# Attention and two feed-forward layers on one core: weight conversions later, and a small add moved from VectorE to GpSimd

## The chip, the cores and the metric

The kernel runs on one core of a Trainium2 chip. The metric is device time in microseconds (us), as the median over runs. TensorE is called PE, VectorE DVE, ScalarE ACT, GpSimd POOL and SyncE SP in the profile, and PEld is TensorE's weight load. A line such as L500 is a line of the kernel before, whose numbers the profile uses.

## The reference

Causal attention with a decay is computed for 4 batches of 8 heads, 576 positions of width 64. Its output, 2304 tokens of width 512, goes through two feed-forward layers.

```
cum    = cumsum(log(clip(f, 1e-4, 1)))            # per head
scores = q @ k.T / 8 + cum[i] - cum[j], masked above the diagonal
e      = exp(scores - rowmax);  attn = e / (sum(e) + 1e-9)
x      = attn @ v                                 # 2304 x 512
y      = (sigmoid(x @ w_gate) * (x @ w_val)) @ w_out      # d_ff 1536
h      = y @ w_in
out    = (h * clip(h + 3, 0, 6) / 6) @ w_out2             # d_ff 2048
```

Here q, k and w_gate are drawn with larger spreads (factors of about 6, 6 and 3.7).

## The kernel before

**Attention.** Two heads of a batch make a pair; there are 16 pairs. Each pair has four units, one for each group of query rows (unit 1 holds two blocks of 128 rows, units 2 and 3 one each, unit 4 the last 64 rows of both heads), so there are 64 units. The main loop has a step t for each unit, and three more. Step t does, in this order: `fixed(t)`, which puts on TensorE, in an order written by hand, the opening of the score banks with a mask, the transposes (`tt`, L220) of the exponentials of unit t-3, the scores (`st`, L216) of unit t, preparation of the next pair's q and k, at most one group of the first feed-forward layer, and, once in a pair, the product with v (`pv`); then `expo(t)`, where VectorE adds the decay to the scores and takes the row minimum (L500) and ScalarE takes the exponential with its sum (L508); then `norm(t)`, below, for unit t-1. Three PSUM banks hold scores, and a unit needs two, so TensorE can open a unit's banks only when VectorE has read (L500) the first bank of the unit before.

**Normalising.** For unit t-1, VectorE adds 1e-9 to the sums (L543, one to four columns of 128 partitions), takes the reciprocal (L544), and GpSimd multiplies the exponentials by it (L546). L543 and L544 are ordered behind VectorE's last read of the scores of unit t, at high priority. `pace["dve"]`, the reciprocal, is what a weight conversion is ordered behind.

**Weight conversions.** Weights of the first layer are read as 64-bit numbers of an odd layout and turned into a high and a low float32r part. The work comes in halves (`Half`) of 128x512 elements: a DMA of 512 KB (L101), four steps to float32 (L107, L108 and L114 on VectorE, L111 on ScalarE between the last two), then the high part (L64 on GpSimd, or L62 on ScalarE) and the low part (L65 on GpSimd). `Converter.run(n, engs)` adds n to a credit and issues one half whenever the credit reaches 1. It is called at the end of each step from t = 4, with `EA` (high part on GpSimd) below t = 16 and `EF` (high part on ScalarE) from there. The first 12 halves are those of the first two groups of 256 features (gate, value, gate, value, out, out: two halves each); when they are done the rate falls to `CS`.

**Filling.** From t = 23 on, `fill.one()` puts one group of the first layer's matmuls (12 of 128x128 by 512) into a step, except mostly the one with `pv`. Three chunks of tokens take 12 groups each: 8 of gate and value (`pg`, `pv`) and then 4 of the product with w_out (`po`). A group whose weights are not converted yet is not issued, and the step stays without one. What is left of the 36 groups after the last unit is issued then, back to back, ahead of the rest of the first layer and the second.

The order on SP's queue is that of the issues; a load that waits for a store holds back the loads behind it. For engines other than TensorE a planner orders instructions by priority and its own estimate of times, and `keep_in_program_order` binds TensorE's.

Of the kernel before, what the change touches and what calls it, by code (L numbers as in the profile page):

```python
# [12 lines left out]
ALU = mybir.AluOpType  # L13
# [7 lines left out]
def attn_moe_kernel(  # L21
# [13 lines left out]
    nc = tc.nc  # L35
# [7 lines left out]
    NQ = 4  # L43
# [150 lines left out]
    conv = Converter()  # L194
# [110 lines left out]
    def behind(i):  # L305
        return tc.issue_after(i.ins) if i is not None else ExitStack()
# [14 lines left out]
    class Pair:  # L321
# [217 lines left out]

        def norm(self, s):  # L540
            m, n = self.m[s], len(self.es[s])
            with behind(reads[-1]), tc.high_priority():
                nc.vector.tensor_scalar(m[:, 8 : 8 + n], m[:, 4 : 4 + n], 1.0e-9, None, ALU.add)  # L543
                pace["dve"] = nc.vector.reciprocal(m[:, 12 : 12 + n], m[:, 8 : 8 + n])  # L544
            for j, e in enumerate(self.es[s]):
                pace["pool"] = nc.gpsimd.tensor_scalar(e, e, m[:, 12 + j : 13 + j], 1.0, ALU.mult, ALU.mult)  # L546
# [504 lines left out]
    class Second:  # L1051
# [93 lines left out]
        def unit(self, k, x, ys, temps, between={}):  # L1145
            u1, u2, p5 = temps
            g, tt = self.ga[k % 2], nc.vector.tensor_tensor
            r11, r22, r12 = self.act(u1, g, 0, 0), self.act(p5, g, 1, 1), self.act(u2, g, 1, 0)
            r21 = self.act(x(), g, 0, 1)
            then = {1: (r11,), 2: (r11,), 3: (r11,), 4: (r22,), 5: (r12, r22, r22), 6: (r21, r12, r12, r21, r21)}  # L1150
            for s in range(7):
                if s in (1, 3):
                    y = ys.pop(0)()
                o = y if s % 2 else x()
                self.product(o, k, s, s in (0, 1, 3))
                if s in (0, 2, 3):
                    nc.scalar.copy({0: u1, 2: u2, 3: p5}[s], o)  # L1157
                elif s < 6:
                    c = {1: u1, 4: p5, 5: u2}[s]
                    tt(c, c, o, ALU.add)  # L1160
                for r in then.get(s, ()):
                    next(r)
                if k % NQ2 == NQ2 - 1:
                    self.load_block(k // NQ2 * 7 + 7 + s)
                if s in between:
                    between[s]()
# [72 lines left out]
    EA = (nc.scalar, nc.gpsimd, nc.gpsimd)  # L1239
    EF = (nc.scalar, nc.scalar, nc.gpsimd)  # L1240
    WU = (8, 4, 4, 4)

    KD, KT, RT = 4, 7, 0

    CA, C0, CB, CC = 0.65, 4, (1.8, 1.0, 1.5, 1.7, 2.0), 1.0

    CE, CS = 0.38, 0.12


    NGA, NCA, GA = 2, 3, 1  # L1250

    NSA = 8
# [111 lines left out]
    for t in range(len(units) + 3):  # L1364
        for job in (fixed, expo, norm, prep):
            job(t)
        if t == 2:
            eight = ep.tile([P, S], F32, tag="e", name="eight")[: B * H]
            nc.vector.tensor_scalar(eight, cum, -8.0, 1.0, ALU.mult, ALU.mult)
            nc.sync.dma_start(cum_d[1], eight)  # L1370
        p, s = unit(t - 4)
        if p and s == p.order[-1] and p.hp == NP - 1 and p.b < NCA:
            done = p.b + 1
        p, s = unit(t - 5)
        if p and s == p.order[-1] and t < len(units) + 3:
            fill.load(p.b, p.hp + 1)
        if t >= C0:
            conv.run(CS if len(conv.jobs) <= 2 * NSA - 6 * NGA else CE if t < NQ * (KT - 1) else CA, EA if t < NQ * KD else EF)
        fill.n = done
    att.close()  # L1380
    pace["dve"] = None
# [63 lines left out]
```

## Time and profile before

| what | value |
|---|---|
| median of 3 runs | 1002.28 us (1002.18 to 1002.36) |
| the profiled execution's own time | 1003.57 us |
| its span in the trace | 1001.8 us |
| mean granted TensorE clock | 0.998 |
| busy share of the span | PE 98%, DVE 53%, ACT 48%, POOL 29% |

The span is from the first to the last instruction of the program on the core. A busy share is an average over stages; the attention stage covers about the first 278 us.

### The profile page before, as it was taken

The numbers are of one execution on the slowest core, as the hardware profiler recorded it, in microseconds if no ns is written. First come the engines' busy times: TensorE is split into PE (matmuls) and PEld (weight loads), VectorE is DVE, ScalarE is ACT, GpSimd is POOL, SyncE is SP. The second block draws the span as 40 slices with busy tenths as digits, with TensorE's granted clock in tenths as the row PEclk, the third lists the DMA queues.
The fourth block names the chain that finished last, engine by engine and source line by source line (L and its number), as shares of the span: only waits on it lengthen the run. The fifth ranks groups of instructions, "written<-read, shape, count | busy, mean of one in ns | idle before, by whom it ended". The sixth has DMA issues, their size and how long they took to land.

```text
span 1001.8 us, 16150 instructions
## 1 busy us (share of the span) xinstructions
PE 986.5 (98%) x5733; PEld 810.4 (81%) x5733; DVE 530.9 (53%) x1220; ACT 476.9 (48%) x1094; POOL 290.5 (29%) x360
## 2 busy tenths in 40 slices
PE   8889999999999999999999999999999999999998
PEld 4556766667688889988888888899899898998987
DVE  6777856645347543737777574553534443333322
ACT  6787677667634432424434343453444443433322
POOL 3675655545323220302334131111111111111110
PEclk9999999999999999999999999999999999999999
DMA  7999796744324352566977578654686845753211
GB/s 184 294 250 226 198 244 156 185 143 145 119 79 154 117 166 82 175 210 264 331 258 252 179 270 318 245 198 166 237 330 206 293 147 193 294 209 148 81 66 64
DMA packets 141072, 197.30 MB, mean 197 GB/s; under 512 B 84192, under 2 KB 93408, under 8 KB 136896
## 3 DMA queue, kind: packets, MB, share of 16 engines
q1 hardware_dynamic: 140944, 196.20, 59.9%
q8 instruction: 45, 0.74, 0.3%
q14 instruction: 35, 0.29, 0.1%
q10 hardware_dynamic: 48, 0.07, 0.0%
HBM read 142.88 MB, written 53.36 MB: 196 GB/s over the span
## 4 chain that ended last, share of the span: by engine, by line
PE 91%; DVE 3%; ACT 2%; DMA 2%; issue 1%; POOL 0%; SPq 0%; DVEq 0%; ACTq 0%; POOLq 0%
PE po L216 34%; PE pv L216 18%; PE u L216 17%; PE pg L216 15%; PE st L216 4%; PE tt L220 3%; DVE e L500 1%; DMA kn<-in_k_dram 1%; ACT e L508 1%; DMA cum_d<-eight 1%; DMA x_d<-x 0%; DVE raw L108 0%; ACT raw L111 0%; ACT etB L580 0%; PE o L216 0%
## 5 line engine op out<-in xcount | busy, mean ns | idle before, releaser
L216 PE MATMUL po<-w,big 128*128 128x512 f32 x864 | 200.5, 390 | 0.0
L216 PEld LDWEIGHTS po<-w,big 128*128 128x128 f32 x864 | 161.8, 188 | 32.8
L216 PE MATMUL pg<-big,wg 128*128 128x512 f32 (+1 forms) x720 | 161.9, 371 | 0.0
L216 PE MATMUL pv<-big,wv 128*128 128x512 f32 (+1 forms) x720 | 161.4, 371 | 0.0
L216 PE MATMUL po<-big,wo 128*128 128x512 f32 (+1 forms) x720 | 160.9, 371 | 0.2 <-DVE big L65 0.2
L216 PEld LDWEIGHTS pg<-big,wg 128*128 128x128 f32 x720 | 125.8, 189 | 27.2 <-issue 4.0
L216 PEld LDWEIGHTS pv<-big,wv 128*128 128x128 f32 x720 | 125.6, 189 | 26.8 <-issue 4.5
L216 PEld LDWEIGHTS po<-big,wo 128*128 128x128 f32 x720 | 125.6, 189 | 25.7 <-issue 2.2
L1160 DVE TENSOR_TENSOR h<-h,u 128x384 f32<-128x384 f32 x69 | 38.2, 554 | 154.0 <-PE u L216 154.0
L546 POOL TENSOR_SCALAR e<-e,m 128x256 f32<-128x256 f32 (+4 forms) x144 | 86.8, 617 | 48.8 <-DVE m L544 32.1
L508 ACT ACTIVATE e<-e,m 128x256 f32<-128x256 f32 (+4 forms) x144 | 83.6, 584 | 31.6 <-DVE m L500 20.3
L216 PE MATMUL u<-h,big 128*128 128x384 f32 x504 | 90.2, 336 | 0.4 <-DVE h L1160 0.4
L216 PE MATMUL u<-h,h 128*128 128x384 f32 x504 | 90.1, 336 | 0.0
L216 PEld LDWEIGHTS u<-h,big 128*128 128x128 f32 x504 | 88.3, 188 | 1.8 <-DVE h L1160 0.8
L216 PEld LDWEIGHTS u<-h,h 128*128 128x128 f32 x504 | 88.4, 188 | 1.0
L1109 POOL TENSOR_TENSOR big<-tail,big 128x384 fp32r<-128x384 f32 x30 | 30.5, 1018 | 196.5 <-PE u L216 115.5
L1157 ACT COPY h<-u 128x384 f32<-128x384 f32 x69 | 32.8, 475 | 111.5 <-PE u L216 111.5
L500 DVE CUSTOM_DVE_ANT_0 e<-st,dc 128x384 f32<-128x384 f32 (+3 forms) x110 | 53.5, 520 | 47.9 <-PE st L216 30.3
L872 DVE SCALAR_TENSOR_TENSOR sg<-sg,pv 128x512 f32<-128x512 f32 (+1 forms) x48 | 29.7, 618 | 92.3 <-PE pv L216 59.7
L111 ACT ACTIVATE raw<-raw 128x512 f32<-128x512 f32 x68 | 45.6, 682 | 67.1 <-DVE raw L108 64.5
L62 ACT CAST big<-sg 128x512 fp32r<-128x512 f32 (+1 forms) x60 | 34.8, 580 | 60.6 <-DVE sg L872 54.6
L114 DVE SCALAR_TENSOR_TENSOR raw<-raw 128x512 int32<-128x512 int32 x68 | 52.5, 782 | 19.4 <-ACT raw L111 18.9
(141 smaller groups left out, 1202.8 us busy)
## 6 DMA issues: line engine op xcount, KB each, us to landing
h<-xc_d SPq DMA_DIRECT2D x21, 768.0 KB, 7.2
big<-x_d SPq DMA_DIRECT2D x28, 512.0 KB, 5.8
raw<-in_moe_w_out_dram SPq DMA_DIRECT2D x28, 512.0 KB, 3.7
h<-wt_d SPq DMA_DIRECT2D x12, 1024.0 KB, 7.4
big<-wt_d SPq DMA_DIRECT2D x12, 1024.0 KB, 7.6
x_d<-x SPq DMA_DIRECT2D x16, 576.0 KB, 3.9
h<-wb_d SPq DMA_DIRECT2D x12, 768.0 KB, 4.6
big<-wb_d SPq DMA_DIRECT2D x12, 768.0 KB, 5.2
```

What stands on the lines that cost most here:

```text
L62: nc.scalar.copy(hi, src)
L111: nc.scalar.activation(e, e, AF.Copy, scale=2.0**-112)
L114: nc.vector.scalar_tensor_tensor(low, high, 3, low, ALU.logical_shift_left, ALU.bitwise_or)
L216: i = nc.tensor.matmul(*a, **k)
L220: i = nc.tensor.transpose(*a)
L500: i = nc.vector.tensor_tensor_reduce(out=e, in0=st, in1=d, op0=ALU.add, op1=ALU.min, scale=self.by, scalar=init, accum_out=m[:, a : a + 1],)
L508: nc.scalar.activation(e, e, AF.Exp, bias=m[:, a : a + 1], scale=-1.0, accum_out=m[:, 4 + b : 5 + b])
L546: pace["pool"] = nc.gpsimd.tensor_scalar(e, e, m[:, 12 + j : 13 + j], 1.0, ALU.mult, ALU.mult)
L872: pace["dve"] = nc.vector.scalar_tensor_tensor(sg, sg, 1.0, pv, ALU.add, ALU.mult)
L1109: (nc.vector if f else nc.gpsimd).tensor_tensor(lo, sg, hi.bitcast(F32), ALU.subtract)
L1157: nc.scalar.copy({0: u1, 2: u2, 3: p5}[s], o)
L1160: tt(c, c, o, ALU.add)
```

## The change

Two edits. The add of 1e-9 is issued on GpSimd, as a tensor_scalar with a multiplication by 1.0 behind the add, at high priority and without an order against VectorE's reads; the reciprocal stays on VectorE. The credit that `Converter.run` gets in a step is 0.24 in place of 0.38, and it changes to 0.65 from t = 21 in place of t = 24. The other rates stay.

```diff
         def norm(self, s):
             m, n = self.m[s], len(self.es[s])
+            with tc.high_priority():
+                nc.gpsimd.tensor_scalar(m[:, 8 : 8 + n], m[:, 4 : 4 + n], 1.0e-9, 1.0, ALU.add, ALU.mult)
             with behind(reads[-1]), tc.high_priority():
-                nc.vector.tensor_scalar(m[:, 8 : 8 + n], m[:, 4 : 4 + n], 1.0e-9, None, ALU.add)
                 pace["dve"] = nc.vector.reciprocal(m[:, 12 : 12 + n], m[:, 8 : 8 + n])
...
-    CE, CS = 0.38, 0.12
+    CE, CS, CT = 0.24, 0.12, 21
...
         if t >= C0:
-            conv.run(CS if len(conv.jobs) <= 2 * NSA - 6 * NGA else CE if t < NQ * (KT - 1) else CA, EA if t < NQ * KD else EF)
+            conv.run(CS if len(conv.jobs) <= 2 * NSA - 6 * NGA else CE if t < CT else CA, EA if t < NQ * KD else EF)
```

## Rows read from the trace of the kernel before

**Rows 1.** The page: busy time, share and instructions of TensorE.

```profile
PE 986.5 (98%) x5733; PEld 810.4 (81%) x5733; DVE 530.9 (53%) x1220; ACT 476.9 (48%) x1094; POOL 290.5 (29%) x360
```

**Rows 2.** Windows: length; busy PE, PEld, DVE, ACT, POOL; clock. Two early pairs; steps 32-34.

```profile
39.09:51.42 12.33, 10.11 (x105) 6.00 (x101) 11.22 (x41) 10.36 (x34) 10.19 (x15) 1.00 1.08 320
...
64.15:76.58 12.43, 10.80 (x114) 6.42 (x111) 10.74 (x40) 11.36 (x36) 8.87 (x12) 1.00 0.92 247
124.53:138.23 13.70, 13.47 (x107) 8.70 (x106) 8.16 (x35) 10.32 (x29) 8.15 (x15) 1.00 0.96 244
```

**Rows 3.** Waits of PE, then of PEld, 24 to 100 us (total, times, longest).

```profile
PE st L216 <- DVE m L500: 3.5, 6, 2.1
PE st L216 <- ACT raw L111: 2.5, 2, 1.4
...
PEld tt L220 <- POOL e L546: 2.3, 5, 0.8
```

**Rows 4.** Timeline (start, us, instruction [idle before]): TensorE opens score banks.

```profile
32.02 0.51 PE L216 MATMUL st<-masks,identb 128*128 128x384 bf16 x2 [2.06 <-DVE m L500]
...
48.18 0.29 PE L216 MATMUL st<-masks,identb 128*128 128x128 bf16 x2 [1.41 <-ACT raw L111]
...
58.19 0.50 PE L216 MATMUL st<-masks,identb 128*128 128x384 bf16 x2 [0.70 <-DVE m L500]
...
63.61 0.29 PE L216 MATMUL st<-masks,identb 128*128 128x128 bf16 x2 [0.18 <-DVE m L500]
...
73.64 0.29 PE L216 MATMUL st<-masks,identb 128*128 128x128 bf16 x2 [1.09 <-ACT raw L111]
```

**Rows 5.** Groups of VectorE, 24.57 to 85.75 us (busy us, mean ns; idle before).

```profile
L108 DVE SCALAR_TENSOR_TENSOR raw<-raw 128x512 int32<-128x512 int32 x7 | 5.9, 839 | 0.1
L114 DVE SCALAR_TENSOR_TENSOR raw<-raw 128x512 int32<-128x512 int32 x7 | 4.8, 692 | 2.2 <-ACT raw L111 2.2
L543 DVE TENSOR_SCALAR m<-m 128x2 f32<-128x2 f32 (+2 forms) x18 | 4.7, 263 | 0.0
...
L107 DVE TENSOR_SCALAR raw<-raw 128x512 int32<-128x512 int32 x7 | 2.9, 408 | 0.0
```

**Rows 6.** Timeline: VectorE idle before L500, units 9, 14, 17 and 22.

```profile
37.46 0.56 DVE L500 CUSTOM_DVE_ANT_0 e<-st,dc 128x384 f32<-128x384 f32 x1 [0.65 <-PE st L216]
...
52.99 0.69 DVE L500 CUSTOM_DVE_ANT_0 e<-st,dc 128x512 f32<-128x512 f32 x1 [1.40 <-POOL e L546]
...
62.99 0.56 DVE L500 CUSTOM_DVE_ANT_0 e<-st,dc 128x384 f32<-128x384 f32 x1 [0.96 <-POOL dt L386]
...
78.06 0.69 DVE L500 CUSTOM_DVE_ANT_0 e<-st,dc 128x512 f32<-128x512 f32 x1 [1.31 <-PE st L216]
```

**Rows 7.** Groups of GpSimd, whole span, shapes kept apart.

```profile
L546 POOL TENSOR_SCALAR e<-e,m 128x512 f32<-128x512 f32 x32 | 25.9, 823 | 6.9 <-DVE m L544 4.5 <-ACT etB L580 1.6 <-PE st L216 0.8
...
L546 POOL TENSOR_SCALAR e<-e,m 128x256 f32<-128x256 f32 x32 | 16.8, 524 | 0.0
```

**Rows 8.** Timeline: GpSimd's low part and VectorE's add at the same time.

```profile
58.18 1.30 POOL L65 TENSOR_TENSOR wv<-raw,wv 128x512 fp32r<-128x512 f32 x1
...
58.73 0.78 DVE L543 TENSOR_SCALAR m<-m 128x2 f32<-128x2 f32 x1
```

**Rows 9.** The chain that ended last: a group after the attention stage (start, us).

```profile
306.10 2.72 PE pg L216 x12
```

**Rows 10.** Timeline of PE: the first two `po` groups, steps 32 and 33.

```profile
126.03 2.80 PE L216 MATMUL po<-big,wo 128*128 128x512 f32 x10
...
129.74 0.59 PE L220 MATMUL tt<-ident,e 64*128 64x64 f32 x12
...
131.17 3.06 PE L216 MATMUL po<-big,wo 128*128 128x512 f32 x12
```

**Rows 11.** Groups of ScalarE, 24.57 to 85.75 us.

```profile
L111 ACT ACTIVATE raw<-raw 128x512 f32<-128x512 f32 x7 | 4.8, 690 | 3.0 <-DVE raw L108 3.0
...
L62 ACT CAST wg<-raw 128x512 fp32r<-128x512 f32 x2 | 1.4, 677 | 0.0
```

## The prediction, made before the change was run

> **What bounds the kernel now.** I began with the page's busy times: TensorE is busy 98% of the span, 986.5 of 1001.8 us [rows 1], so what can be won by removing waits is small. The windows show where the missing time lies. Two early pairs, steps 9 to 12 and 17 to 20, take 12.33 and 12.43 us, and TensorE's busy time in them is 10.11 and 10.80; at the same time VectorE has 11.22 and 10.74, ScalarE 10.36 and 11.36, GpSimd 10.19 and 8.87 [rows 2]. Here no engine is full and all are close: the pace is set by who waits for whom. The waits of TensorE in 24 to 100 us say for whom: 3.5 us for VectorE's L500, 2.5 us put down to ScalarE's L111, and its weight loads 2.3 us for GpSimd's multiplications [rows 3]. The 2.5 us are the same wait in disguise: both gaps stand before an opening of score banks (1.41 and 1.09 us), which needs L500, and L111 is what happened to end just then [rows 4]. From step 23 on, the groups of the first layer fill TensorE's stream, and there TensorE is the bound.
>
> So a saving before step 23 counts in full, as long as the next engine does not take it; one behind step 23 counts only where TensorE has nothing to fill in.
>
> **The change, part by part.** First the count, since the rates alone don't tell it. Adding the credit step by step, the halves are issued today at the end of steps 6, 9, 11, 14, 17, 19, 22, 24, 26, 27, 29 and 30; afterwards at 8, 12, 16, 20, 22, 23, 25, 27, 28, 30, 31 and 33. Before the first group at step 23 that is seven halves now and five then, and the twelfth comes three steps later. Each moved half takes its 512 KB load on SP's queue, three VectorE steps, L111 and the two parts with it.
>
> *(a) Early conversions.* One half costs VectorE 0.41 + 0.84 + 0.69 = 1.94 us [rows 5]. In today's kernel the four large gaps of TensorE before an opening, 2.06, 1.41, 0.70 and 1.09, each follow a conversion (those of steps 6, 11, 14 and 19), while an opening with none before it waits 0.18 [rows 4]. The excess is 5.26 - 4 x 0.18 = 4.5 us. The halves of steps 9 and 17 leave no such gap. Afterwards the first four halves all come at the first unit of a pair, where today none is. VectorE sits idle shortly behind these places for 0.65, 1.40, 0.96 and 1.31 us [rows 6], 4.3 us in all, against 4 x 1.94 = 7.8 us to place; 3.4 us are left, part of which falls in the pv groups' shadow, as for steps 9 and 17. I charge a third of it, 1.1 us: -4.5 + 1.1 = **-3.4 us**. Bounds: -4.5 (all hidden), and +3.0 (each of the four new places as dear as the dearest old one, 4 x (2.06 - 0.18) - 4.5).
>
> *(b) The add.* L543 takes 4.7 us in 18 instructions of the early stretch [rows 5]. TensorE waited for VectorE 6.0 us of 76 [rows 3], about a tenth, so I take a tenth: **-0.4 us**, with -4.7 as the lower bound, if all of it were on the path. GpSimd's price for an add on 1 to 4 columns is not in the trace; its multiplications of 512 and 256 columns take 823 and 524 ns [rows 7], a straight line that would leave 0.23 us at no columns. It is above nothing and below 0.52; I take 0.23. It adds a wait: the reciprocal now waits for GpSimd, and behind it on VectorE stand the next conversion and the next L500, for which TensorE waits. What hides it: the exponentials' sums are ready one unit before the reciprocal may run, since that is ordered behind L500 of the following unit. If the cover is gone, the cost goes to the five waits of the weight loads for GpSimd and their likes [rows 3]: 5 x 0.23 = 1.2 us as upper bound of the add's own time; a queue in front of it is a rival below. Past step 23 the add lies beside TensorE's groups, and its removal from VectorE too, so both are nothing there.
>
> One row bears on where the add lies: L543 took 0.78 us and ended with GpSimd's L65, which ran 58.18 to 59.48 beside it [rows 8]; the mean of 263 ns in this stretch [rows 5] holds such cases. The Trainium skill (SBUF — State Buffer, section "SBUF: two separate sides") says that the two engines share a port pair under an exclusive lock, held for a whole instruction. By that rule the add on GpSimd could itself hold up VectorE, at worst 18 x 0.23 = 4.1 us; a tenth of that would make this term 0.0 in place of -0.4. The rest of the sum stands without it.
>
> *(c) The hole in the filling.* Gate and value groups need halves 2, 4, 6 and 8, and by the count each finds them ready. The first po group needs the twelfth: today it is there for step 32, afterwards only for step 35 (34 holds pv). Steps 32 and 33 stay without a group, and two groups more are left for the end, 3 in place of 1, each at 2.72 us [rows 9]: +5.44. What the two steps give back is less than the groups' 3.71 (126.03 to 129.74) and 3.06 us [rows 10], as the other engines are now uncovered. The stretch of steps 32 to 34 takes 13.70 us; without the groups TensorE alone needs 6.9. ScalarE has 10.32 us of work there [rows 2], and the halves of steps 31 and 33 come in with 0.69 + 0.68 us each (L111 and L62 [rows 11]); less two copies out for the groups, of L62's size, that is 11.7. VectorE gets 8.16 + 2 x 1.94, less four adds of 0.26, 11.0. The nearest case is the early pace without groups, (12.33 + 12.43) / 8 = 3.1 a step [rows 2], 9.3 for three. It saves 4.4: 5.44 - 4.4 = **+1.0 us**. Bounds: -1.4 (6.9) and +3.4 (11.7).
>
> Loads: two fetches fewer sit on SP's queue before step 23 and two more at steps 31 and 33, ahead of loads that a pair needs a unit or more later. At the end, two chunks' loads of the next tokens wait for the last gate group, which comes two steps later; three left-over groups (8.2 us) cover them. I cost this at nothing; uncovered, it would be one load's landing, below the bounds above.
>
> Sum: -3.4 - 0.4 + 1.0 = -2.8 us, from the profiled execution's 1003.57 to 1000.8; that execution lies 1.3 above the median, so the median goes from 1002.28 to **999.5 us**.
>
> **The rivals.**
> *Other engines take the early gain.* ScalarE has 11.36 of 12.43 us in the pair of steps 17 to 20 [rows 2], and TensorE's weight loads already wait for GpSimd; against it, its own waits are mostly for VectorE. If only a third of (a) stays, -1.1 - 0.4 + 1.0 = -0.5: 1001.8 us.
> *The hole takes it all.* ScalarE's 11.7 us set steps 32 to 34: -3.8 + 3.4 = -0.4: 1001.9 us. For it speaks that two conversions fall right there; against it, that exponentials run two units ahead of their transposes.
> *GpSimd holds the reciprocal (slower).* The add lands behind a 1.30 us L65 [rows 8] or a run of multiplications. If it comes 0.65 us late, half an L65, at 9 of the 18 early units, VectorE stands 5.9 us, and the sum is +3.1: 1005.4 us. It decides from 4.8 us of such holding (the gain of 2.8 and 2.0 more), 0.27 for each early reciprocal; below that the result is not slower. GpSimd's 2 to 3 us of free time in a pair speak against it. The Trainium skill (GPSIMD Engine Reference, section "Performance versus the Vector engine") advises elementwise work to stay on VectorE; that is this case.
> *The new places are dear.* All four as the dearest old one: +3.0 - 0.4 + 1.0 = +3.6: 1005.9 us. The idle times [rows 6] speak against it.
> That the change doesn't do what it says is not among them: the count shows the moves, and the add has nowhere else to go.
>
> **How the numbers follow.** A measurement here can tell about 0.2%, 2.0 us, from no change. My forecast (a gain over 2.0) gets 0.45, centred on 999.5, with a range of its own from 995.5 to 1000.3. The engines that take the gain get 0.20 and the hole 0.13, both within 2.0 us: 0.33. The held reciprocal gets 0.15 and the dear places 0.07: 0.22 slower. The range starts at 995.5 (sum of the better bounds of (a) and (c) near -6, and a little of the add) and must reach into the slower cases to leave out no more than 2 in 10: 995.5 to 1005.0. The planner's new order of the other instructions, which no row shows, is in that width.
>
> **What would show it.** In the profile after: conversions beginning behind the reciprocals of units 7, 11, 15 and 19, openings before step 23 without gaps over about 0.5 us, and step 23's group some 3 to 4 us earlier: (a) right. L543's place empty on VectorE, 64 short instructions on GpSimd, and no idle time before L544 put down to them: (b) right. No po group in steps 32 and 33, three left after the attention stage, and steps 32 to 34 in 9 to 10 us: (c) right. A reciprocal that sits idle for GpSimd, an opening with a gap behind the four new places, or ScalarE without a pause in steps 32 to 34 would make the prediction wrong.

## The result, and the profile after

The changed kernel takes **1009.92 us** (median of 6 runs, 1008.07 to 1012.36); the kernel before, run on the same chip, takes 1002.32 us (6 runs, 1001.17 to 1005.44). The ratio is **1.0072**, with a 95% interval of 1.0053 to 1.0092: slower by 0.7%. The forecast was 999.5 us with a range from 995.5 to 1005.0, so the range misses it, and the sign is wrong. The profiled execution has a span of 1008.0 us against 1001.8, which is the 6.2 us that the rows below divide up. Among the kernels below, one of the 12 runs of kernel 14 took 1392.29 us at a mean clock of 0.654, and its ratio leaves that run out.

The page of the changed kernel shows the moved add, and that TensorE has no less to do. VectorE has 64 instructions and 12.0 us less than before, GpSimd 62 instructions and 11.6 us more [rows 1]: 64 adds, less the high parts of two halves, which now come after step 15 and so fall to ScalarE.

```profile
PE 989.3 (98%) x5733; PEld 811.6 (81%) x5733; DVE 518.9 (51%) x1156; ACT 477.9 (47%) x1096; POOL 302.1 (30%) x422
```

Windows of the changed kernel (length; busy PE, PEld, DVE, ACT, POOL; clock, DMA share, GB/s). First the stretches that answer to [rows 2] (the pairs from reciprocal to reciprocal), then two short ones after the pause of step 23, and two in the empty steps:

```profile
36.58:48.89 12.31, 10.80 (x117) 6.61 (x119) 9.43 (x34) 10.22 (x33) 9.73 (x17) 1.00 0.90 254
61.40:73.91 12.51, 11.00 (x117) 6.60 (x119) 8.74 (x35) 11.09 (x35) 8.82 (x16) 1.00 0.89 219
124.71:138.61 13.90, 10.29 (x82) 5.33 (x82) 10.16 (x28) 10.08 (x24) 10.50 (x17) 0.75 0.87 220
...
84.50:86.50 2.00, 1.96 (x9) 0.91 (x11) 0.00 (x0) 0.81 (x2) 0.00 (x0) 0.68 0.72 279
86.50:88.50 2.00, 2.00 (x21) 1.35 (x19) 0.69 (x1) 1.61 (x4) 0.27 (x1) 0.50 1.07 329
...
130.71:132.71 2.00, 0.67 (x6) 0.36 (x6) 1.31 (x4) 1.54 (x6) 2.00 (x4) 0.50 1.11 238
132.71:134.71 2.00, 1.91 (x14) 1.04 (x14) 1.06 (x3) 1.34 (x4) 1.66 (x6) 0.50 0.71 111
```

VectorE's work in the early pairs fell by 1.8 and 2.0 us, and the pairs are as long as before: 12.31 and 12.51 against 12.33 and 12.43. Steps 32 to 34 hold two groups less and take 13.90 against 13.70 us.

TensorE's timeline in the changed kernel says where it stood:

```profile
36.23 0.29 PE L216 MATMUL st<-masks,identb 128*128 128x128 bf16 x2 [1.29 <-DVE m L500]
...
48.55 0.28 PE L216 MATMUL st<-masks,identb 128*128 128x128 bf16 x2 [1.36 <-DVE m L500]
...
84.54 1.12 PE L216 MATMUL pg<-big,wg 128*128 128x512 f32 x3 [2.41 <-DMA big<-x_d]
85.46 0.86 PE L216 MATMUL st<-masks,identb 128*128 128x384 bf16 x2
...
128.79 0.58 PE L220 MATMUL tt<-ident,e 64*128 64x64 f32 x12 [2.19 <-ACT etB L581]
...
131.38 0.37 PE L220 MATMUL tt<-ident,e 64*128 64x64 f32 x2 [0.52 <-ACT etB L581]
132.57 1.27 PE L220 MATMUL tt<-ident,e 64*128 64x64 f32 x10 [0.81 <-POOL e L547]
```

Three things are to be seen. An opening still waits 1.29 to 1.36 us behind each of the four new conversion places (two are shown; the others are at 61.05 and 73.56). The first group of the first layer, in step 23, stops in its last quarter for the load of x. And the empty steps are not short but full of pauses. Where the first scores of a step start, against the profile of before, gives the account: step 23 is 3.17 us early, step 24 is 0.28 late, steps 25 to 32 are 0.14 to 0.18 late, step 35 is 0.38 late. Then two groups more are left for the end (36 matmuls of the filling instead of 12 after the attention stage), 2 x 2.72 [rows 9] = 5.44 us, and 0.4 us come on the rest of the way: 0.40 + 5.44 + 0.4 = 6.2.

### The profile page after: what moved, and what is told of

Read it like the earlier page. It is cut to its first block, busy times and chain, and to the rows that moved or that the text cites. A ratio compares the mean times of both kernels' runs of the same rounds, so it can differ in the third digit from the quotient of the medians.

```text
span 1008.0 us, 16122 instructions
## 1 busy us (share of the span) xinstructions
PE 989.3 (98%) x5733; PEld 811.6 (81%) x5733; DVE 518.9 (51%) x1156; ACT 477.9 (47%) x1096; POOL 302.1 (30%) x422
## 4 chain that ended last, share of the span: by engine, by line
PE 92%; POOL 2%; DVE 2%; issue 2%; DMA 1%; ACT 0%; SPq 0%; POOLq 0%; DVEq 0%; ACTq 0%
PE po L216 34%; PE pv L216 18%; PE u L216 17%; PE pg L216 14%; PE st L216 5%; PE tt L220 3%; POOL e L547 1%; POOL dt L386 1%; PE o L216 1%; DVE e L500 1%; DVE raw L108 0%; DMA big<-x_d 0%; DMA kn<-in_k_dram 0%; DVE xp L891 0%; POOL m L543 0%
## 5 line engine op out<-in xcount | busy, mean ns | idle before, releaser
L111 ACT ACTIVATE raw<-raw 128x512 f32<-128x512 f32 x68 | 45.4, 679 | 64.8 <-DVE raw L108 62.5
L500 DVE CUSTOM_DVE_ANT_0 e<-st,dc 128x384 f32<-128x384 f32 (+3 forms) x110 | 53.3, 519 | 42.9 <-PE st L216 42.3
```

Source lines behind the costliest of these rows:

```text
L111: nc.scalar.activation(e, e, AF.Copy, scale=2.0**-112)
L500: i = nc.vector.tensor_tensor_reduce(out=e, in0=st, in1=d, op0=ALU.add, op1=ALU.min, scale=self.by, scalar=init, accum_out=m[:, a : a + 1],)
```

## The experiments

Fifteen kernels were timed against the kernel before, each with its ratio to the runs of its own chip. The last columns come from the timelines: the start of the first scores of a step, in us against the profile of before (81.87, 103.55, 125.17 and 138.59), and the groups left for the end.

| Kernel | Median us (runs) | Ratio, 95% interval | Step 23 | 27 | 32 | 35 | Left |
|---|---|---|---|---|---|---|---|
| changed kernel | 1009.92 (6) | 1.0072 [1.0053, 1.0092] | -3.17 | +0.18 | +0.18 | +0.38 | 3 |
| 1 add only | 1005.53 (8) | 1.0031 [1.0020, 1.0043] | -2.13 | +1.50 | +1.50 | +1.34 | 1 |
| 2 conversions only | 1011.76 (4) | 1.0092 [1.0077, 1.0107] | -2.80 | -0.77 | -0.69 | +1.41 | 3 |
| 3 empty steps only | 1006.86 (6) | 1.0048 [1.0034, 1.0062] | -1.58 | -1.67 | -1.67 | -3.19 | 3 |
| 4 rate 0.75 | 1012.57 (4) | 1.0105 [1.0090, 1.0121] | -3.62 | +3.09 | +3.09 | +7.18 | 1 |
| 5 x load first | 1012.70 (6) | 1.0100 [1.0081, 1.0119] | -3.46 | +2.55 | +2.55 | +4.06 | 3 |
| 6 add till unit 19 | 1002.69 (12) | 1.0004 [0.9991, 1.0018] | -2.86 | +0.76 | +0.76 | +0.76 | 1 |
| 7 late till step 17 | 1008.43 (6) | 1.0060 [1.0043, 1.0076] | +0.40 | +4.44 | +4.44 | +4.43 | 1 |
| 8 empty steps 56, 57 | 1004.26 (12) | 1.0015 [1.0004, 1.0027] | -1.35 | -1.87 | -1.87 | -1.87 | 3 |
| 9 change, mask late | 1009.00 (6) | 1.0079 [1.0059, 1.0099] | -3.66 | -2.31 | -2.31 | +0.07 | 3 |
| 10 before, mask late | 1002.03 (11) | 0.9997 [0.9988, 1.0005] | +0.02 | -0.87 | -0.87 | -0.90 | 1 |
| 11 add, mask late | **1000.48** (11) | **0.9980** [0.9972, 0.9989] | -2.35 | -3.25 | -3.25 | -3.43 | 1 |
| 12 change, both waits gone | 1006.88 (5) | 1.0054 [1.0042, 1.0066] | -3.05 | -3.22 | -3.22 | -0.65 | 3 |
| 13 both gone, late till 17 | 1002.82 (12) | 1.0003 [0.9992, 1.0014] | -2.20 | -2.34 | -2.34 | -2.52 | 1 |
| 14 empty, conversions done | 1005.15 (12) | 1.0027 [1.0015, 1.0038] | -1.12 | -1.14 | +0.06 | -4.20 | 3 |
| 15 both gone, rate 0.85 | 1009.90 (6) | 1.0076 [1.0058, 1.0094] | -2.99 | +0.57 | +2.75 | +3.07 | 1 |

One caution is read off first. Up to step 23 the kernel before and kernels 3, 8, 10 and 14 run the same program (10 differs by one instruction behind it), and they reach step 23 at 81.87, 80.29, 80.52, 81.89 and 80.75 us. So a difference before step 23 is good to 1.6 us only; what is lost between two steps of one profile is not touched by that. These differences all arise up to step 9: from the first scores of step 9 to those of step 23 the five keep their distances within 0.1 us. In that stretch the six kernels with both halves of the change (the change, 4, 5, 9, 12 and 15) gain 0.2 us each, the three with the add alone (1, 6 and 11) 0.4, and kernel 2 with the conversions alone loses 0.3. The windows of the kernel before show a low clock from 30 to 40 us:

```profile
30.00:40.00 10.00, 7.80 (x72) 4.78 (x74) 7.65 (x30) 8.01 (x27) 6.10 (x10) 0.83 1.11 295
```

The gap of 2.06 us [rows 4] on which the prediction leaned is 1.18 in kernel 3, 1.45 in kernel 8 and 1.26 in kernel 14, and the granted clock of kernel 3 there is 1.00 (first row of its windows, below); in kernel 10 it is 2.02. Part of the gain that the prediction expected was the misfortune of the execution it was read from.

### The two halves of the change, and the hole (1 to 4)

**1, the add alone** on the kernel before:

```diff
+            with tc.high_priority():
+                nc.gpsimd.tensor_scalar(m[:, 8 : 8 + n], m[:, 4 : 4 + n], 1.0e-9, 1.0, ALU.add, ALU.mult)
             with behind(reads[-1]), tc.high_priority():
-                nc.vector.tensor_scalar(m[:, 8 : 8 + n], m[:, 4 : 4 + n], 1.0e-9, None, ALU.add)
```

> Only the add moves to GpSimd; the conversions stay as before. Theory (the loss is a late load of x at step 23 and the two steps without a group; the add is harmless): within 1.5 us of before. Rival (the reciprocal held by GpSimd is the loss): 4 us or more slower than before.

By the medians it is 3.35 us slower, between theory and rival. It loses 3.6 us between steps 23 and 27. GpSimd's timeline there:

```profile
86.24 0.41 POOL L449 TENSOR_SCALAR_AFFINE_SELECT dz<-dc 128x256 f32<-128x256 f32 x1 [5.85 <-DMA dc<-cum_d]
86.62 1.31 POOL L65 TENSOR_TENSOR wv<-raw,wv 128x512 fp32r<-128x512 f32 x1
...
90.70 0.19 POOL L543 TENSOR_SCALAR m<-m 128x1 f32<-128x1 f32 x1
```

and VectorE's:

```profile
90.92 0.17 DVE L545 RECIPROCAL m<-m 128x1 f32<-128x1 f32 x1 [4.28 <-POOL m L543]
```

The reciprocal is held, as the slower rival had it, but most of it at one place: 4.28 us here, against 3.1 us in eight waits from 24 to 84 us. GpSimd's queue stands 5.85 us for a load, and the add is the sixth instruction behind it. A conversion and the next L500 stand behind the reciprocal, and TensorE behind those.

**2, the conversions alone:**

```diff
-    CE, CS = 0.38, 0.12
+    CE, CS, CT = 0.24, 0.12, 21
...
-            conv.run(... CE if t < NQ * (KT - 1) else CA, ...)
+            conv.run(... CE if t < CT else CA, ...)
```

> Only the conversions move; the add stays on VectorE. Theory: most of the loss, 5 to 8 us slower than before, with steps 32 and 33 empty and the first group of step 23 waiting for x or arriving no earlier. Rival (held reciprocal): within 2 us of before.

It is 9.6 us slower than before by the medians, more than the theory's 5 to 8, and no faster than the whole change (1.0092 against 1.0072, with intervals that meet). It loses 2.0 us between steps 23 and 27, 2.1 in steps 32 to 34, and leaves three groups.

**3, the hole alone:** the kernel before, without a group in steps 32 and 33.

```diff
-        if t > NQ * (NP + 1) + 2 and not (last and p.i != NP + 1 and t < len(units)):
+        if t > NQ * (NP + 1) + 2 and t not in (32, 33) and not (last and p.i != NP + 1 and t < len(units)):
```

> The kernel before with steps 32 and 33 left without a group and nothing else changed; no conversion is issued near them after step 30. If empty steps as such give nothing back: 5 us slower than before. If the conversions of steps 30 to 33 in the empty steps are what eats it: 1 to 2 us slower, with steps 32 to 34 in about 10 us.

The two steps give back 3.19 - 1.67 = 1.5 us of the 5.44 that the two groups cost later: 3.9 us net in the profile, 4.7 by the medians. TensorE's timeline:

```profile
127.72 0.90 PE L220 MATMUL tt<-ident,e 64*128 64x64 f32 x12 [2.97 <-ACT etB L580]
128.38 2.05 PE L216 MATMUL st<-kp,qp 64*128 64x512 f32 x4
```

A pause of 2.97 us for ScalarE's copy, and scores that take 2.05 us behind it, at a granted clock of 0.66 and then 0.50, as the windows of kernel 3 show:

```profile
30.00:40.00 10.00, 8.27 (x86) 4.79 (x88) 8.79 (x35) 8.30 (x27) 7.39 (x11) 1.00 1.09 290
...
126.86:128.86 2.00, 1.14 (x14) 1.17 (x16) 1.53 (x7) 1.59 (x5) 0.22 (x1) 0.66 1.03 223
128.86:130.86 2.00, 2.00 (x16) 0.87 (x12) 0.29 (x1) 0.73 (x2) 1.41 (x4) 0.50 1.16 292
```

**4, the change with a faster rate from step 21 on** so that the twelfth half is there in time and no step is empty:

```diff
-    CA, C0, CB, CC = 0.65, 4, (1.8, 1.0, 1.5, 1.7, 2.0), 1.0
+    CA, C0, CB, CC = 0.75, 4, (1.8, 1.0, 1.5, 1.7, 2.0), 1.0
```

> The changed kernel with a credit of 0.75 from step 21, so that the twelfth half comes at step 31 and no step stays without a group. Theory: 4.5 to 6 us faster than the changed kernel, 2 to 3 slower than before, since the late load of step 23 stays. If the empty steps don't matter: as the changed kernel, 7 us slower than before.

The hole was gone and the kernel was no faster (1.0105 against 1.0072). The output groups came close on the conversion of their weights, as TensorE's timeline shows:

```profile
132.65 0.50 PE L216 MATMUL po<-big,wo 128*128 128x512 f32 x1 [1.09 <-ACT wo L62]
...
134.99 0.61 PE L216 MATMUL po<-big,wo 128*128 128x512 f32 x1 [1.00 <-POOL wo L65]
```

but 6.7 us had been lost before, between steps 23 and 27, so the first question was what happens there.

### What takes the early gain back (5 to 7, 9 to 12)

In the changed kernel SP's queue shows the wait for x of step 23 (start, time of issue):

```profile
72.81 4.88 SPq L352 DMA_DIRECT2D qn<-in_q_dram  x4
77.79 1.81 SPq L352 DMA_DIRECT2D kn<-in_k_dram  x2
79.70 0.44 SPq L205 DMA_DIRECT2D big<-x_d  x1
```

Two loads of pair 8's keys stand ahead of the load of x; in the kernel before all four stood behind it, and it was issued at 76.93. **5** puts pair 8's loads behind it (`ring` keeps the load's instruction):

```diff
+                with behind(ring[0, KC - 1]) if self.i == KT + 1 else ExitStack():
-                self.qn, self.kn = (self.load_blocks(new(nm), src) for nm, src in (("qn", q), ("kn", k)))
+                    self.qn, self.kn = [self.load_blocks(new(nm), src) for nm, src in (("qn", q), ("kn", k))]
```

> The changed kernel, with the loads of the ninth pair (pair 8, counted from 0) put behind the fourth load of x in the queue. Theory (at step 24 the changed kernel loses 3.4 us of its early gain because the first group of the first layer waits 2.41 us for an x load that is queued behind two loads of pair 8, and TensorE's clock then falls): the gap before that group is under 0.5 us, steps 24 to 32 start about 3 us earlier than in the changed kernel, and the end comes 2.5 to 3.5 us earlier, near 1006.5 to 1007.5 median, because the hole of two steps is left. Rival (the step 24 loss is what any early gain meets there, since the other engines are full, and the load is only the wait that happened to be seen): the gap moves to another engine and the end stays within 1 us of the changed kernel's 1009.9.

The wait fell from 2.41 to 0.14 us, and step 24 came 3.3 us earlier, as the theory said. From step 25 on all of it was gone, and more by step 27. In step 24 TensorE waits for a multiplication:

```profile
91.14 1.35 PE L220 MATMUL tt<-ident,e 64*128 64x64 f32 x16 [3.55 <-POOL e L548]
```

VectorE's reciprocal waits for the add:

```profile
93.41 0.16 DVE L546 RECIPROCAL m<-m 128x1 f32<-128x1 f32 x1 [6.92 <-POOL m L544]
```

and both stand behind GpSimd, which waits with the same mask as in kernel 1 (its line is L450 here):

```profile
88.75 0.41 POOL L450 TENSOR_SCALAR_AFFINE_SELECT dz<-dc 128x256 f32<-128x256 f32 x1 [8.76 <-DMA dc<-cum_d]
```

**6** is kernel 1 with the add on GpSimd for pairs 0 to 4 only (units 0 to 19):

```diff
+            if self.i < 5:
                 with tc.high_priority():
                     nc.gpsimd.tensor_scalar(m[:, 8 : 8 + n], m[:, 4 : 4 + n], 1.0e-9, 1.0, ALU.add, ALU.mult)
             with behind(reads[-1]), tc.high_priority():
+                if self.i >= 5:
+                    nc.vector.tensor_scalar(m[:, 8 : 8 + n], m[:, 4 : 4 + n], 1.0e-9, None, ALU.add)
```

> The kernel before, with the add on GpSimd for pairs 0 to 4 (units 0 to 19) and on VectorE from unit 20 on. Theory (with the add alone on GpSimd the early stretch gains about 0.5 us and steps 25 to 27 lose 3.9, where the add stands on GpSimd behind a wait of 5.85 us for the decay's transfer and four other instructions, the reciprocal waits 4.28 us for it, and TensorE's clock falls after the pause): the loss at steps 25 to 27 is gone and the end is at or up to 1 us before the kernel before: 1001.3 to 1002.5 median. Rival (the loss at steps 25 to 27 belongs to the shifted order of the early stretch, and the reciprocal is only where it shows): the end stays 2 us or more later, near 1005.

Its time came near the theory's, and its steps refute the theory: it still loses 3.6 us between steps 23 and 27, though the add is on VectorE there. VectorE is not held any more:

```profile
86.11 0.16 DVE L548 RECIPROCAL m<-m 128x1 f32<-128x1 f32 x1
```

but GpSimd is, and its multiplications, for which TensorE waits 2.44 us at 90.19, come late all the same:

```profile
87.36 0.41 POOL L449 TENSOR_SCALAR_AFFINE_SELECT dz<-dc 128x256 f32<-128x256 f32 x1 [7.89 <-DVE raw L108]
```

(The releaser named is only what ended last, at 87.32. The load of `dc` was issued at 81.27, 6.1 us before; in kernel 1 it was issued at 80.55 and the mask began 5.7 us later.) So it is not the add that holds VectorE, but the mask that holds everything on GpSimd. **7** is kernel 2 with the late rate of conversions up to step 17 only, so that from step 22 on they come as before:

```diff
-    CE, CS, CT = 0.24, 0.12, 21
+    CE, CS, CT = 0.24, 0.12, 17
```

> The kernel before, with the late rate of conversions kept only up to step 17: halves at the end of steps 8, 12, 16, 18, 19, 21, 22, 24, 26, 27, 29, 30, so that from step 22 on they are as in the kernel before; the add stays on VectorE. Theory (the changed conversions lose at two places, the x load at step 23 that the shifted loads delay and the twelfth half that comes three steps late): no step without a group, one group left at the end, and with the early gain of 1 to 2 us partly kept the end is 0 to 1.5 us before the kernel before: 1000.8 to 1002.3 median. Rival (the loss lies in the crowded conversions behind step 17 themselves): steps 18 to 23 lose what the first three places gained, and the end is 1 to 3 us later than before.

By the medians it is 6.4 us slower, more than the rival's 1 to 3. It loses 2.7 us on steps 18 to 23, the rival's case, and 4.0 again between 23 and 27: here the load of `dc` was issued at 83.80, and the mask began at 91.04.

That mask, L449 with `dz`, belongs to pair 7 and is needed in step 31. The planner puts it into GpSimd's queue before the multiplications of unit 22. **9** moves this one instruction behind the multiplications of unit 28; up to 295 us nothing else changes its place on VectorE, ScalarE or GpSimd. **10** does it to the kernel before, **11** to kernel 1, and **12** to kernel 5, so that both waits are gone from the change (0.43 us of the wait for x is left):

```diff
         if s == 2:
-            p.hide(0)
+            with behind(pace["pool"]) if p.i == UP else ExitStack():
+                p.hide(0)
```

> The changed kernel, with one GpSimd instruction moved: the first mask of pair 7 (dz<-dc, L449), which stands in GpSimd's queue before the multiplications of unit 22 and waits there 7.93 us for the load of pair 7's decay although it is needed only in step 31, goes behind the multiplications of unit 28. Theory (the early gain is held back at steps 24 to 26 by transfers: GpSimd stands in front of this mask until the decay's load lands, and what stands behind it, the second part of a weight half, two multiplications and the add, holds VectorE and TensorE; that load does not come earlier when the steps do): the idle time of 7.9 us is gone, and steps 26 to 32 start 0.5 to 2 us earlier than in the changed kernel, whose larger wait at step 24 is for the x load and stays. End 1008 to 1009.5 median. Rival (the wait is harmless, since TensorE has the first groups to run meanwhile): no step moves by more than 0.3 us, median within 0.7 of 1009.9.

> The kernel before, with the same one instruction moved. It waits 6.09 us there, and behind it TensorE waits 0.64 us at 91.69 us for a multiplication. Theory: 0.3 to 0.8 us earlier from step 25 on, 1001.3 to 1002 median, too little to tell from no change by the median alone, so it is read from the steps. Rival (harmless): the steps stay.

> The kernel before with the add on GpSimd (the first experiment), and the same one instruction moved. Theory (the 3.9 us that the add alone lost at steps 25 to 27 come from this mask: the add stood behind it and four more instructions, and the reciprocal, the next conversion and the next openings stood behind the add): the loss is gone, steps 27 to 63 start 3 to 4 us earlier than in the first experiment, and the end is 0 to 2 us before the kernel before: 1000.5 to 1002.3 median. Rival (the add as such holds the reciprocal, behind whatever GpSimd has there): steps 27 on gain under 1 us, median near 1005.

> The changed kernel with both waits on transfers taken away: the ninth pair's loads behind the x load (as in the fifth experiment, whose gain of 3.3 us at step 24 went again at step 25 in a wait of 3.55 us for GpSimd and a lower clock) and the mask of pair 7 late. Theory (two transfers, x and decay, are all that took the early gain back): steps 25 to 32 start 2 to 3.5 us earlier than in the changed kernel, only the hole is left, and the end is 1006.5 to 1008.5 median, before the changed kernel and 4 us or more before the fifth experiment. Rival (the early gain always goes at the next engine): steps 26 to 32 start within 0.7 us of the changed kernel's, median 1009 or more.

All four went the theory's way in the steps, three by somewhat more than it had said: at step 27 by 2.5 us for 9, 0.9 for 10 and 4.7 for 11, and by 3.4 for 12, as said. Kernel 9's time can't be told from the change's (1.0079 against 1.0072): it loses 2.4 us again in the hole. In the add's kernel GpSimd works through (11, GpSimd's timeline):

```profile
81.87 1.31 POOL L65 TENSOR_TENSOR wv<-raw,wv 128x512 fp32r<-128x512 f32 x1 [1.69 <-ACT wv L62]
...
86.34 0.19 POOL L543 TENSOR_SCALAR m<-m 128x1 f32<-128x1 f32 x1
```

The loss of 3.6 us between steps 23 and 27 has become a gain of 0.9, and **the add on GpSimd with the mask late is faster than both kernels**: 0.9980 [0.9972, 0.9989] of before, 5 us before kernel 1. It is the add that does this, not the mask: ten of kernel 11's eleven runs (1000.16 to 1000.73 us) lie below the fastest of the eleven of kernel 10, which has the mask alone (1000.81). The mask alone gains 0.9 us at step 25 of the kernel before, which the medians can't tell. In kernel 12 nothing is lost between steps 23 and 27: the two transfers took all of the early gain back. At step 32 it stands at -3.22, kernel 11 at -3.25: as far as two profiles can tell, moving the conversions adds nothing to what the add and the mask give.

### What the hole costs (8, 13 to 15)

From step 32 on kernel 12 has only the hole, and loses by it: three steps take 2.6 us longer than with two groups in them, and 5.44 us are left for the end. ScalarE's timeline:

```profile
124.84 0.66 ACT L111 ACTIVATE raw<-raw 128x512 f32<-128x512 f32 x1 [2.24 <-DVE raw L108]
125.41 1.05 ACT L582 COPY etB<-tt 128x512 f32<-128x512 f32 x2
```

and TensorE's:

```profile
126.61 0.91 PE L220 MATMUL tt<-ident,e 64*128 64x64 f32 x12 [3.42 <-ACT etB L582]
```

The copy that frees the transposes' bank stands behind a step of a conversion, and that waits for VectorE's L108, in front of which stand the two transposes of the next pair's q and k (L399 and L400, 122.80 to 124.16). **8** puts the hole of kernel 3 where no conversion falls:

```diff
-        if ... and t not in (32, 33) and ...:
+        if ... and t not in (56, 57) and ...:
```

> The kernel before, with no first-layer group in steps 56 and 57, where no conversion falls, instead of 32 and 33 as in the third experiment. Theory (steps 32 and 33 gave back only 1.5 of their groups' 6.8 us because transposes of the next pair, a conversion and the copy of a weight half stood in queue there, and the clock fell): here the two steps give back 4 us or more of the two groups' time, two groups more at the end cost 5.4, and the end is 0.5 to 1.5 us later than before: about 1003 median. Rival (two steps without a group cost that much wherever they are, since the other engines set the pace uncovered and TensorE's clock falls): the end is 3.5 to 5 us later, about 1006 to 1007, with a granted clock near 0.5 to 0.7 in the two steps.

There the steps give back 4.2 us, and the hole costs 5.44 - 4.2 = 1.2 in the profile, 2.2 by the medians. **14** is kernel 3 with the rate from step 24 on at 0.9, so that the twelfth half is done at step 28 and the hole has no conversion beside it:

```diff
-    CA, C0, CB, CC = 0.65, 4, (1.8, 1.0, 1.5, 1.7, 2.0), 1.0
+    CA, C0, CB, CC = 0.9, 4, (1.8, 1.0, 1.5, 1.7, 2.0), 1.0
```

> The kernel before with no group in steps 32 and 33 (the third experiment), and a faster rate of conversions from step 24 on (0.9 for 0.65), so that the twelfth half comes at the end of step 28 and no conversion stands near the two empty steps. Theory (steps 32 and 33 gave back only 1.5 us there, against 4.2 in steps 56 and 57, because the last two halves were being converted in them: ScalarE's copies for the transposes stood behind a half's part, and TensorE paused 2.97 us and lost its clock): steps 32 to 35 give back 3.5 to 4.5 us, and no pause above 1 us. Rival (it is the place: the change of batch, the two loads, or the next pair's transposes): they give back 2 us or less, with a pause of over 2 us. The end may be off by what six conversions in as many steps cost at steps 24 to 28; it is read by steps.

Steps 32 to 34 give back 4.3 us in place of 1.5, with pauses of 0.68 and 0.96 us on TensorE and no loss of clock, as the theory said:

```profile
125.23:134.39 9.16, 7.40 (x79) 4.28 (x76) 5.56 (x23) 7.42 (x19) 5.29 (x12) 1.00 0.79 182
```

Of these 4.3 us, 1.2 make up for what steps 29 to 31 had lost, where the conversions are crowded, so the net is 3.1 against 1.5. The theory had read the pause of kernel 3 as a copy that stood behind a half's part. ScalarE's timelines of kernel 3 and of kernel 14 show what stands in front of the copy:

```profile
125.98 0.62 ACT L62 CAST big<-sg 128x512 fp32r<-128x512 f32 x1 [1.12 <-DVE sg L726]
...
125.42 0.62 ACT L62 CAST big<-sg 128x512 fp32r<-128x512 f32 x1 [1.43 <-DVE sg L726]
```

In both it is the product of the last gate and value groups, which waits for VectorE's L726. In kernel 3 L726 stands behind the next pair's two transposes (123.96 to 125.32), in kernel 14 it waits 0.16 us for the value group. The copy starts at 126.51 in kernel 3 and at 125.94 in kernel 14, 0.57 us earlier, while TensorE starts step 32 at 123.51 and 125.23, 1.72 us later. So 1.72 of the 2.29 us by which the pause is shorter are TensorE's own lateness. In kernel 8 the same two transposes stand in step 56, with no such product in front of the copy, and the pause is 0.81 us. The order of the costs is this: a hole costs 1.2 us in steps 56 and 57, 2.4 in steps 32 and 33 with the conversions done at step 28 (5.44 - 3.06), 3.9 with the last of them at step 30, and 5.6 to 8.0 in the kernels that have the change's halves at steps 30, 31 and 33 (the change, 2, 5, 9 and 12).

**13 and 15** are kernel 12 with no hole, by the late rate up to step 17 only (13), or by a rate of 0.85 from step 21 on (15):

```diff
 13:
-    CE, CS, CT = 0.24, 0.12, 21
+    CE, CS, CT = 0.24, 0.12, 17
 15:
-    CA, C0, CB, CC = 0.65, 4, (1.8, 1.0, 1.5, 1.7, 2.0), 1.0
+    CA, C0, CB, CC = 0.85, 4, (1.8, 1.0, 1.5, 1.7, 2.0), 1.0
```

> The changed kernel without its two waits for transfers (the ninth pair's loads behind the x load, pair 7's first mask late), and with the late rate of conversions kept only up to step 17, so that the twelfth half comes at the end of step 30 as in the kernel before. Theory (with the transfers out of the way the hole is all that is left of the loss): no step without a group, steps 25 to 63 start 2.5 to 3.5 us before the kernel before, and the end is 1 to 2.5 us before it: 1000 to 1001.5 median, 5 to 6.5 us before the changed kernel without the two waits but with the hole. Rival (weights that come just in time make new waits wherever the conversions are moved later): steps 18 to 35 lose 2 us or more, median 1003 to 1007.

> The changed kernel without its two waits for transfers, conversions as in the change up to step 23 (four by the first group), and a rate of 0.85 for 0.65 from step 21 on: the rest at the end of steps 24, 25, 26, 27, 29 and 30. Theory (as for the run with the late rate up to step 17): no hole, 1000 to 1001.5 median. Rival (weights just in time: the first groups wait for the halves they need, as in the run with rate 0.75, which lost 4.3 us at steps 26 to 33 and 1.1 behind them): waits of the gate, value and output groups for just-converted weights, median 1004 or more. If this one is slow and the other fast, it is the later conversions themselves that cost.

13 is 4 to 5 us faster than kernel 12 (4.1 by the medians, 0.5% by the ratios) and level with before; its early part lost 1.4 us at steps 18 to 22, where the conversions are crowded, which falls between theory and rival. 15 loses 5.2 us between steps 24 and 32, where a half comes in nearly every step. TensorE's timeline:

```profile
93.57 0.28 PE L216 MATMUL st<-masks,identb 128*128 128x128 bf16 x2 [1.09 <-DVE m L501]
94.84 0.53 PE L220 MATMUL tt<-ident,e 64*128 64x64 f32 x10 [0.98 <-ACT etB L582]
...
109.58 0.59 PE L220 MATMUL tt<-ident,e 64*128 64x64 f32 x12 [1.49 <-ACT etA L582]
```

None of the waits shown is one of a group for its weights, which the rival named; they are openings and transposes behind conversions. Halves that are put off must be caught up in steps that have no room for them, or leave the filling with a hole.

## Why the prediction was wrong, by its own steps

The forecast of -2.8 us and the profile's +6.2 lie 9.0 us apart: 4.64 for the hole, 3.35 for the loads, 0.6 for the early gain (-3.17 where -3.4 and -0.4 were forecast) and 0.4 behind the attention stage, which was not in the sum.

**The hole, term (c), is the step that failed most.** It was put at +1.0 us, with +3.4 as the upper bound, from the early pace without groups, 3.1 us a step. It measured 0.20 (steps 32 to 34) + 5.44 = +5.64. The count of steps and groups was right: steps 32 and 33 empty, three groups left. The price holds where no conversion is near (1.2 us in kernel 8). The prediction counted the late halves in those steps as work (11.7 us for ScalarE as the bound) and not the order in which it stands: etB's copy behind L111, that behind L108, and L108 behind the next pair's two transposes. TensorE paused 2.19 and 0.52 us for such copies and 0.81 us for a multiplication that stood on GpSimd behind a half's L65, and its clock was 0.50 for what came next. The stretch went to 13.90 us, beyond every engine's sum.

**The loads, costed at nothing, took the early gain.** The prediction looked at SP's queue for the end of the attention stage and for steps 31 and 33. It did not ask which load is next due when everything up to step 23 comes earlier. In the profile the changed kernel lost 3.35 us between steps 23 and 27, to the load of x; with that wait gone, to the load of pair 7's decay (kernel 5), and with both gone, nothing (kernel 12).

**The early conversions, term (a),** gained too little, and at one place only. The four new places cost 1.29 + 1.36 + 1.36 + 1.36 = 5.4 us of openings, what the four old ones cost (5.26 us [rows 4]). VectorE's idle times [rows 6] did not hide them, and L108, priced at 0.84 us, took 1.11 in each (last section). What is gained lies ahead of step 9, where the half of step 6 is gone from in front of the longest gap: there the six kernels with both halves of the change are 2.8 to 3.5 us early, and the other executions of the program of before 0.1 to 1.6. Against those five executions step 23 is 1.6 to 3.2 us early, with the add's part in it; -3.8 was predicted for both, and that one profile shows -3.17 is in part luck.

**The add, term (b),** was right early, where it gains 0.4 us between steps 9 and 23, and wrong behind step 23, where the prediction called it nothing because TensorE has groups to run. In the stretch that it argued from, 24 to 84 us, the reciprocal waited 1.7 us in 5 places for the add in the changed kernel. At step 24 of kernel 1 it waited 4.28 us at once. With the mask out of the way the add gains: kernel 11 lies 1.55 us under kernel 10 by the medians, their intervals just meeting at 0.9988 and 0.9989. The Trainium skill (GPSIMD Engine Reference, section "Performance versus the Vector engine") would keep such work on VectorE. Here the measurement decides otherwise for an add on 1 to 4 columns, which took 192 ns on GpSimd in kernel 11 (row below).

**The rivals.** "GpSimd holds the reciprocal" was the mechanism in kernel 1, with a cause that it did not name: not a multiplication or L65 in front of the add, but an instruction that waits for a transfer. "The hole takes it all" was the right place at +3.4 for 5.64. "The new places are dear" had them at 2.06 us each, and they were 1.3. "Other engines take the early gain" came true by way of the transfers.

**What would show it:** conversions behind the reciprocals of units 7, 11, 15 and 19, the add's 64 instructions on GpSimd, and the count of groups came as said. Openings without gaps, steps 32 to 34 in 9 to 10 us, and a reciprocal that never waits did not.

What stays open: why kernel 14's steps lose 1.2 us between 29 and 31 was read as crowding and not tested, and how the loss in steps 32 and 33 divides between the late halves, the next pair's transposes and the product of the groups was not separated. That the late halves make the hole dearer is shown only as the order of the costs above.

## What to carry to other kernels

When work is made earlier, look in the profile for the next instruction that waits for a transfer on an in-order queue, and list what stands behind it: a load does not come earlier because its user does, and here one early mask on GpSimd held VectorE and TensorE too. Price an empty place by the order of what stands in it, not by the sum of each engine's work; a delay that falls on the critical engine's own release (a copy behind a conversion step or a cast) costs the pause, and in kernel 3 and the changed kernel the clock as well. And move a thing on its own before judging it: here one part of a slower change, with one waiting instruction put back, beats both kernels.

## What the runs showed of the hardware

**VectorE's conversion step L108 and GpSimd's instructions hold each other up.** The mean of L108 in 24.57 to 85.75 us was 839 ns before [rows 5]. In the changed kernel's groups (busy us, mean ns):

```profile
L108 DVE SCALAR_TENSOR_TENSOR raw<-raw 128x512 int32<-128x512 int32 x6 | 6.3, 1052 | 0.2
L543 POOL TENSOR_SCALAR m<-m 128x2 f32<-128x2 f32 (+2 forms) x18 | 5.0, 280 | 1.6
```

and in those of kernel 11, with the halves in the old places:

```profile
L108 DVE SCALAR_TENSOR_TENSOR raw<-raw 128x512 int32<-128x512 int32 x7 | 5.1, 730 | 0.1
L543 POOL TENSOR_SCALAR m<-m 128x2 f32<-128x2 f32 (+2 forms) x18 | 3.5, 192 | 1.5
```

The single instructions say why. The timelines of GpSimd and VectorE in the changed kernel, at the first of the new places, and an L108 beside which GpSimd is idle:

```profile
34.40 0.77 POOL L547 TENSOR_SCALAR e<-e,m 128x576 f32<-128x576 f32 x1 [0.37 <-PE st L216]
34.59 1.11 DVE L108 SCALAR_TENSOR_TENSOR raw<-raw 128x512 int32<-128x512 int32 x1
35.25 0.51 POOL L543 TENSOR_SCALAR m<-m 128x4 f32<-128x4 f32 x1
...
83.44 0.69 DVE L108 SCALAR_TENSOR_TENSOR raw<-raw 128x512 int32<-128x512 int32 x1
```

L108 takes 0.69 us where GpSimd is idle as it begins. Where a GpSimd instruction is running, it takes 0.69 us and what is then left of that instruction beyond 0.15 us: 0.70 us with 0.15 left, 0.74 with 0.20, 0.95 with 0.41, 1.06 with 0.52, and 1.11 with 0.57. In the 17 profiles, from 24.57 to 140 us, 200 of 204 come within 0.03 us of this. The other way round, the add on GpSimd takes 0.19 us alone and 0.51 where it begins during L108. At each of the four new places a multiplication of 128x576 has 0.57 us left, and the add follows: 0.42 us more for L108 and 0.32 for the add. At the old places L108 took 0.74 to 1.07 in the kernel before. The Trainium skill (SBUF — State Buffer, section "SBUF: two separate sides") says that GpSimd and a VectorE instruction with two inputs from SBUF shut each other out of a shared port pair. These rows agree with that.

**TensorE's clock after a pause.** After 2.41 us without work in the changed kernel (step 23) the granted clock was 0.68 and then 0.50, the level of 1.2 GHz, and the scores of step 24 took 1.59 in place of 0.87 us. After 1.96 us at the same place in kernel 9 it stayed at 1.00, the level of 2.4 GHz, in the windows:

```profile
83.58:85.58 2.00, 2.00 (x23) 1.36 (x25) 0.38 (x1) 0.99 (x2) 1.75 (x3) 1.00 0.86 275
```

From step 23 to step 24 the wait for x cost 3.4 us in the first, 1.0 more than the wait, and 2.2 in the second, 0.3 more. Why the clock fell in one and not in the other is not shown.

**Identical programs differ by 1.6 us at step 23** from one execution to the next, all of it arising up to step 9, with a clock of 0.83 in the kernel before and 1.00 in kernel 3 in 30 to 40 us. A forecast made from one profile's gaps takes that chance for a property of the kernel.
